# Layer 2 of a three-part fp32 kernel: loads of x2 in parts, another bend, longer transfers in the planner

## The chip, the cores and the metric

One NeuronCore of a Trainium2 chip runs the whole program. The metric is the device time of one execution in microseconds (us); before the change the median of 3 runs is 1015.37 us (1014.89 to 1016.47). Engines: PE (TensorE, matmuls), DVE (VectorE), ACT (ScalarE), POOL (GpSimd) and SP (SyncE, which issues DMAs).

## The reference

Attention over 4 batches, 8 heads, 576 positions, width 64, followed by two feed-forward layers on the 2304 tokens x 512 features that come out of it. All is float32.

```python
# attention: causal softmax, and a read of a memory, mixed by a gate
local = softmax(causal(q @ k.T / 8)) @ v
mem_out = (phi(q) @ M_prev) / (phi(q) @ z_prev + 1e-6)      # phi(x) = elu(x) + 1
x = g * mem_out + (1 - g) * local                           # 2304 x 512
# layer 1: w_in 512 x 2048, w_out 2048 x 512, scalars s and b
r = np.maximum(x @ w_in, 0.0)
x = (s * (r * r) + b) @ w_out
# layer 2: weights of the same shapes; the "bend"
h = x @ w_in
g = np.where(h >= 1, h, np.where(h <= -1, 0.0, (h + 1) ** 2 / 4))
out = g @ w_out
```

## The kernel before

Every fp32 operand of a matmul is kept as two halves, a rounded one (hi) and the rest (lo), and each product is three matmuls: hi·hi, hi·lo and lo·hi. Making the halves takes a rounding (`rnd`, ACT L536, DVE L537 or POOL L541) and a subtraction (`sub`, DVE L528 or POOL L532).

The order of all work comes from a planner in Python (`Plan`, L110 to 347). The kernel's code only records operations with their reads, writes, a priority (ATT before FFN before W2) and for each a list of "ways": the engines that could do it, with a cost in us. `Plan.order` simulates the engines with these costs, picks for each operation the engine, and gives one fixed order for each engine. An engine works strictly in that order: an instruction that waits holds up all behind it. The same holds for SP, whose queue issues nearly all DMAs (`dma`, L507; issued at L510): a DMA that must wait for a buffer or for data holds up the DMAs behind it. In the simulation, transfers follow one another at 335 GB/s, with 1.3 us ahead and 1.3 us behind each (DMA_START, DMA_END). Where the planner expects PE to stand idle it inserts small filler matmuls (L1298).

Layer 1 works on blocks of 256 tokens (the last, "wide", has 512) and leaves its result x2, scaled by s, in DRAM (x2d, one tensor for a block; L978). The term with b is the same for all tokens: b times the column sums of w_out. `column_sums` adds up the 32 halves of w_out in the tile mask (31 adds, L1032), sums over the partitions with four 128x1 matmuls (L1038) and keeps the result in cs (L1040).

Layer 2 works on 5 blocks of tokens (BLOCKS2: block 0 has 256 and is done plainly; blocks 1 to 4 have 512 and use Strassen's seven products), in two passes over the hidden units: FIRST, blocks 0, 1, 2, 3, 4 with half of the hidden units, then SECOND, blocks 4, 1, 2, 3, 0 with the other half. For each block `load_x2` (L1065) brings x2 from x2d to the tile xr, as one DMA for each block of layer 1 (two for a 512 token block); `x2_sums` (L1098) adds cs (ACT L1106 or POOL L1108), forms Strassen's sums (L1116, L1117) and makes their halves in xx (and gg). `products` (L1170 to 1172) multiplies with the weights in wi, `strassen` (L1181) combines the products in wif and wof, `bend` (L1142 to 1161) applies the bend and makes halves in wo and g, and `second` multiplies with w_out (L1202, L1203 with the rounded half, L1209 with the rest). The first pass stores its partial results (yd), the second loads them back (st<-yd), adds (DVE L1275) and stores out (out_dram<-st, L1278). During the first pass `prepare` (L664) converts the weights of the second: raw loads, roundings and subtractions (L594 to 605, L692, L714), stores to w2d; `bring` (L720) loads these later.

The bend before, for h in src: DVE clips h to -1..1 (L1152), ACT squares 0.5·clip + 0.5 (L521), DVE takes the larger of h (or clip) and the square (L1156, L1158).

Of the kernel before, what the change touches and what calls it, by code (L numbers as in the profile page):

```python
# [109 lines left out]
class Plan:  # L110
# [116 lines left out]
    def line(self, keys):  # L227
# [50 lines left out]
        while n_out < len(ops):  # L278
# [44 lines left out]
            if len(o.way) > 3:  # L323
                dma = max(dma, free[e] + self.DMA_START) + o.way[3]
                o.ends = ("SP", dma + self.DMA_END)
# [50 lines left out]
def tile_kernel(ctx: ExitStack, tc: tile.TileContext, qk_in, nv_in, z_prev, beta,  # L376
# [105 lines left out]
    R_RW = Pool([lambda i=i: made["xr"][:, i:i + 512] for i in (1024, 1536)] + [rr[:, 0:512]])  # L482
# [24 lines left out]
    def dma(dst, src, nbytes, r=(), w=(), pr=2, acq=(), late=False):  # L507
        small = pr in (ATT, LOAD)
        last = (nbytes / (240e3 if small else 335e3),)
# [154 lines left out]
    def prepare(p):  # L664
# [4 lines left out]
        def put(k, make):  # L669
# [7 lines left out]
            dma(lambda: w2d[p, k // 2][:, 512 * j:512 * j + 512], lambda: sg.t, P * 2048, [sg], [f"w2d{p}_{k // 2}"], W2)  # L677
# [23 lines left out]
        for i in range(2):  # L701
# [6 lines left out]
            for k in (8 + 2 * i, 9 + 2 * i):  # L708
# [272 lines left out]
    def layer1_step(bi, fi, ys):  # L981
# [6 lines left out]
        old = ["narrow"] * (wide and fi > 1)  # L988
        plan.phase = 1 if wide else None

        def rv(r=r):
# [4 lines left out]
            [hs] + old, [r], FFN, [r])  # L996
# [25 lines left out]
    def column_sums():  # L1022
# [16 lines left out]
        pe(1.0, go, ["mask", "sb"], [z], W2, [z])  # L1039
        dve(0.1, lambda: nc.vector.tensor_scalar(cs_t, z.t[:, 0:NK], con[:, 1:2], None, ALU.mult), [z, "sb"], ["cs"], W2)  # L1040
# [36 lines left out]

    def x2_plain():

        load_x2(0, lambda: made["xr"][:, 0:NK * T].rearrange("p (c n) -> p c n", c=NK))  # L1080
        for kt in range(NK):
# [6 lines left out]
            def lo(kt=kt):  # L1088
# [5 lines left out]
                ["xr", "cs"], [f"xp{kt}"], FFN)  # L1094
            dve(c_dve(T), lambda kt=kt, xv=xv, hi=hi, lo=lo: nc.vector.scalar_tensor_tensor(
                lo(), xv(), col(kt), f(hi()), ALU.add, ALU.subtract), ["xr", "cs"], [f"xp{kt}"], FFN)

    def x2_sums(bi):  # L1098
# [3 lines left out]
        load_x2(bi, xr)  # L1102
        for kt in range(NK):
            def xv(kt=kt):
# [4 lines left out]
                ["xr", "cs"], [f"xr{kt // 2}{j}" for j in range(2)], FFN)  # L1109
# [4 lines left out]
        def tt(i, j, a, c):  # L1114
# [251 lines left out]
```

## Time and profile before

| | |
|---|---|
| median of 3 runs | 1015.37 us (1014.89 to 1016.47) |
| the profiled execution | 1018.43 us, its span 1016.6 us |
| granted clock of PE, mean | 0.991 of full speed |
| busy: PE | 998.8 us, 98% of the span |
| DVE, ACT, POOL | 679.8, 571.0, 192.3 us |
| the chain that ended last | PE 86%, ACT 8%, DMA 3%, DVE 1% |

The profile is one execution, recorded by the hardware, and 3.06 us longer than the median of the timed runs. The span runs from the first to the last recorded instruction. "Busy" sums what an engine spent in instructions; PE's matmuls overlap, so a busy PE may still run at a low clock. The clock is given as a share of 2.4 GHz; its lower level is 1.2 GHz.

### The profile page before, as it was taken

What the parts mean: (1) busy time and instruction counts of PE and PEld (TensorE: products, weight loads), DVE (VectorE), ACT (ScalarE), POOL (GpSimd) and SP (SyncE); (2) the same over time, 40 slices, a digit from 0 to 9 for tenths busy, and PEclk for the clock granted to TensorE, in tenths of its full rate; (3) what the DMA queues carried; (4) which work ended last, traced back from release to release, by engine and by line L of the source; (5) the groups of instructions that cost most, each with busy time, mean ns of one, the idle gap of its engine ahead of it and who ended that gap; (6) DMA issues with size and microseconds to landing.
All of it is one profiled execution on the core that took longest, in us unless ns stands there. A gap on an engine that the chain in (4) does not pass through costs nothing.

```text
span 1016.6 us, 19496 instructions
## 1 busy us (share of the span) xinstructions
PE 998.8 (98%) x7484; PEld 882.8 (87%) x7484; DVE 679.8 (67%) x1597; ACT 571.0 (56%) x1301; POOL 192.3 (19%) x298
## 2 busy tenths in 40 slices
PE   8999999999999999999999999999999999989997
PEld 7799998898898898888998889989899899878886
DVE  5999855625744635644878967988797458666753
ACT  5999876746646655645565556555554233433322
POOL 5411133211110211101112213412321001211001
PEclk8999999999999999999999999999999999998999
DMA  9590034212122121220133347454426832130311
GB/s 324 195 410 21 22 95 139 73 35 81 46 74 62 61 66 50 84 66 21 71 118 105 125 151 241 145 161 154 154 94 243 314 127 86 40 125 1 104 31 32
DMA packets 50302, 115.57 MB, mean 114 GB/s; under 512 B 5024, under 2 KB 15776, under 8 KB 50208
## 3 DMA queue, kind: packets, MB, share of 16 engines
q1 hardware_dynamic: 49984, 113.72, 32.8%
q8 instruction: 59, 0.97, 0.4%
q0 software_dynamic: 224, 0.59, 0.3%
q14 instruction: 35, 0.29, 0.1%
HBM read 87.56 MB, written 26.74 MB: 112 GB/s over the span
## 4 chain that ended last, share of the span: by engine, by line
PE 86%; ACT 8%; DMA 3%; DVE 1%; issue 1%; SPq 0%; POOL 0%; DVEq 0%; ACTq 0%; POOLq 0%
PE hb L950 6%; PE hb L952 6%; PE hb L951 6%; PE ab L825 6%; PE yb L1013 5%; PE yb L1018 5%; PE yb L1014 5%; PE ab L904 4%; PE ab L880 4%; PE ab L1202 3%; PE yb L1202 3%; PE ab L1203 3%; PE yb L1203 3%; PE yb L1209 3%; PE ab L1209 3%; PE hb L1170 2%
## 5 line engine op out<-in xcount | busy, mean ns | idle before, releaser
L950 PE MATMUL hb<-xx,wi 128*128 128x256 f32 (+1 forms) x512 | 152.7, 298 | 0.1
L951 PE MATMUL hb<-xx,wi 128*128 128x256 f32 (+1 forms) x512 | 149.6, 292 | 0.0
L952 PE MATMUL hb<-xx,wi 128*128 128x256 f32 (+1 forms) x512 | 149.6, 292 | 0.0
L1013 PE MATMUL yb<-gg,wo 128*128 128x256 f32 (+1 forms) x394 | 102.4, 292 | 0.3 <-POOL gg L541 0.3
L950 PEld LDWEIGHTS hb<-xx,wi 128*128 128x128 f32 x512 | 96.3, 188 | 7.1 <-issue 3.5
L951 PEld LDWEIGHTS hb<-xx,wi 128*128 128x128 f32 x512 | 96.4, 188 | 2.8
L952 PEld LDWEIGHTS hb<-xx,wi 128*128 128x128 f32 x512 | 96.2, 188 | 2.9
L1014 PE MATMUL yb<-gg,wo 128*128 128x256 f32 (+1 forms) x394 | 98.0, 281 | 0.0
L528 DVE TENSOR_TENSOR gg<-rr,gg 128x256 fp32r<-128x256 f32 (+1 forms) x105 | 46.2, 442 | 76.0 <-ACT gg L536 56.4
L521 ACT ACTIVATE aa<-aa,sm 128x384 f32<-128x384 f32 (+4 forms) x112 | 69.4, 621 | 48.6 <-DVE sm L836 48.4
L521 ACT ACTIVATE wif<-wif,con 128x512 f32<-128x512 f32 x46 | 33.1, 721 | 87.4 <-DVE wif L1152 87.3
L836 DVE CUSTOM_DVE_ANT_0 aa<-ab,mask 128x512 f32<-128x512 f32 (+3 forms) x112 | 59.1, 553 | 32.9 <-PE ab L825 32.6
L1013 PEld LDWEIGHTS yb<-gg,wo 128*128 128x128 f32 x394 | 74.1, 188 | 7.4 <-issue 3.6
L1014 PEld LDWEIGHTS yb<-gg,wo 128*128 128x128 f32 x394 | 74.2, 188 | 0.4
L994 ACT ACTIVATE rr<-hb 128x256 f32<-128x256 f32 (+1 forms) x102 | 40.9, 401 | 56.7 <-PE hb L952 55.5
L1018 PE MATMUL yb<-gg,wo 128*128 128x256 f32 (+1 forms) x394 | 69.1, 288 | 0.0
L825 PE MATMUL ab<-qk 64*64 64x512 f32 (+5 forms) x320 | 58.3, 471 | 0.0
L1018 PEld LDWEIGHTS yb<-gg,wo 128*128 128x128 f32 x394 | 54.5, 188 | 2.2 <-issue 1.8
L1171 PE MATMUL ab<-xx,wi 128*128 128x256 f32 x192 | 54.1, 282 | 2.4 <-POOL xx L532 2.4
L1170 PE MATMUL ab<-xx,wi 128*128 128x256 f32 x192 | 54.0, 281 | 0.0
L1170 PE MATMUL hb<-xx,wi 128*128 128x256 f32 x192 | 54.0, 281 | 0.0
L1171 PE MATMUL hb<-xx,wi 128*128 128x256 f32 x192 | 54.0, 281 | 0.0
(337 smaller groups left out, 2838.4 us busy)
## 6 DMA issues: line engine op xcount, KB each, us to landing
w2d<-st SPq DMA_DIRECT2D x48, 256.0 KB, 3.4
nv<-in_nv_dram SPq DMA_DIRECT2D x16, 576.0 KB, 3.7
wir<-in_moe_w_in_dram SPq DMA_DIRECT2D x16, 512.0 KB, 10.2
wor<-in_moe_w_out_dram SPq DMA_DIRECT2D x16, 512.0 KB, 10.1
raw<-in_moe_w_in_dram SPq DMA_DIRECT2D x16, 512.0 KB, 3.6
raw<-in_moe_w_out_dram SPq DMA_DIRECT2D x16, 512.0 KB, 4.1
qk<-in_qk_dram SPq DMA_DIRECT2D x16, 448.0 KB, 3.3
xr<-x2d SPq DMA_DIRECT2D x14, 512.0 KB, 4.9
```

Of the source, the lines that this page charges most:

```text
L521: nc.scalar.activation(o(), i(), func, **{a: b() if callable(b) else b for a, b in kw.items()})
L825: nc.tensor.matmul(zs[x].t[own if t == 4 else slice(0, n), at:at + c1 - c0], qk.t[own, q0:q0 + n], qk.t[own, k0 + c0:k0 + c1], start=True, ...
L950: nc.tensor.matmul(o, w_in_part(fi, 0)[:, kt, :], x_h(kt), start=kt == 0, stop=False)
L951: nc.tensor.matmul(o, w_in_part(fi, 0)[:, kt, :], x_l(kt), start=False, stop=False)
L952: nc.tensor.matmul(o, w_in_part(fi, 1)[:, kt, :], x_h(kt), start=False, stop=kt == NK - 1)
L1013: nc.tensor.matmul(yv(c), w_out_part(fi, 0)[:, cs], gg.t[0], start=fi == 0 and c % k == 0, stop=False)
L1014: nc.tensor.matmul(yv(c), w_out_part(fi, 1)[:, cs], gg.t[0], start=False, stop=False)
L1018: pe(c_mm(n), lambda c=c, cs=cs, gg=gg, fi=fi: nc.tensor.matmul(yv(c), w_out_part(fi, 0)[:, cs], gg.t[1], start=False, stop=fi == NF - 1 a ...
L1170: nc.tensor.matmul(o, sw(q, k, 0, kt), xo(k, 0, kt), start=j == 0 and kt == 0, stop=False)
L1171: nc.tensor.matmul(o, sw(q, k, 0, kt), xo(k, 1, kt), start=False, stop=False)
L1202: nc.tensor.matmul(y.t, gh.t[:, cs], wo2(q, i, 0), start=first and jj == 0, stop=False)
L1203: nc.tensor.matmul(y.t, gh.t[:, cs], wo2(q, i, 1), start=False, stop=False)
```

## The change

Four edits, all in the source of one file; lines behind L1065 move down by 10.

1. The planner assumes longer transfers: 2.5 us more until the data of a w2d store or load, a yd store or load or a store of out count as landed, and 1.5 us more for a load of x2.
2. The load of a block of x2 into xr is split: for each of the two blocks of layer 1 one DMA for features 0 to 255 (256 KB) and two of 128 KB; and xr is tracked in 8 cells (feature chunk, token half) and no longer as one. Only the last chunk waits for the wide block of layer 1, whose spare buffers fall from three to two.
3. The bend: ACT makes relu(0.5·h + 0.5) and squares it, and DVE makes min(max(h, 1), square) in one operation.
4. The matmuls of the column sums get a higher priority, and one wait of the wide block's relu starts one step earlier.

```diff
@@ Plan.order
             if len(o.way) > 3:
                 dma = max(dma, free[e] + self.DMA_START) + o.way[3]
-                o.ends = ("SP", dma + self.DMA_END)
+                o.ends = ("SP", dma + self.DMA_END + o.way[4])
@@
-    R_RW = Pool([lambda i=i: made["xr"][:, i:i + 512] for i in (1024, 1536)] + [rr[:, 0:512]])
+    R_RW = Pool([lambda: made["xr"][:, 1536:2048], rr[:, 0:512]])
@@
-    def dma(dst, src, nbytes, r=(), w=(), pr=2, acq=(), late=False):
+    def dma(dst, src, nbytes, r=(), w=(), pr=2, acq=(), late=False, wait=0.0):
         small = pr in (ATT, LOAD)
-        last = (nbytes / (240e3 if small else 335e3),)
+        last = (nbytes / (240e3 if small else 335e3), wait)
@@ prepare: the store of w2d (one of two), and in the same way bring, the loads of yd, the stores of yd and out
-                dma(lambda k=k: w2d[p, k // 2][:, 512 * (k % 2):512 * (k % 2) + 512], lambda sg=sg: sg.t, P * 2048, [sg], [f"w2d{p}_{k // 2}"], W2)
+                dma(lambda k=k: w2d[p, k // 2][:, 512 * (k % 2):512 * (k % 2) + 512], lambda sg=sg: sg.t, P * 2048, [sg], [f"w2d{p}_{k // 2}"], W2, wait=2.5)
@@ layer1_step
-        old = ["narrow"] * (wide and fi > 1)
+        old, old_r = (["narrow"] * (wide and fi > x) for x in (1, 0))
...
-            [hs] + old, [r], FFN, [r])
+            [hs] + old_r, [r], FFN, [r])
@@ column_sums
-        pe(1.0, go, ["mask", "sb"], [z], W2, [z])
-        dve(0.1, lambda: nc.vector.tensor_scalar(cs_t, z.t[:, 0:NK], con[:, 1:2], None, ALU.mult), [z, "sb"], ["cs"], W2)
+        pe(1.0, go, ["mask", "sb"], [z], ATT, [z])
+        dve(0.1, lambda: nc.vector.tensor_scalar(cs_t, z.t[:, 0:NK], con[:, 1:2], None, ALU.mult), [z, "sb"], ["cs"], FFN)
@@
-    def load_x2(bi, view):
+    def cells(kts, js=(0, 1)):
+        return [f"xr{kt}_{j}" for kt in kts for j in js]
+
+    def load_x2(bi):
 
         p0, p1 = BLOCKS2[bi]
         for l1, (a, e) in enumerate(BLOCKS):
             s, t = max(a, p0), min(e, p1)
-            if s < t:
-                dma(lambda s=s, t=t: view()[:, :, s - p0:t - p0],
-                    lambda l1=l1, s=s, t=t, a=a: x2d[l1].rearrange("c p n -> p c n")[:, :, s - a:t - a],
-                    P * NK * (t - s) * 4, [f"x2d{l1}"] + ["wide"] * (bi > 0), ["xr"], W2)
+            if s >= t:
+                continue
+            if not bi:
+                dma(lambda: made["xr"][:, 0:NK * T].rearrange("p (c n) -> p c n", c=NK),
+                    lambda: x2d[0].rearrange("c p n -> p c n"), P * NK * T * 4, ["x2d0"], cells((0, 1)), W2, wait=1.5)
+                continue
+            for k0, k1 in ((0, 2), (2, 3), (3, 4)):
+                dma(lambda s=s, t=t, k0=k0, k1=k1: made["xr"].rearrange("p (c n) -> p c n", c=NK)[:, k0:k1, s - p0:t - p0],
+                    lambda l1=l1, s=s, t=t, a=a, k0=k0, k1=k1: x2d[l1].rearrange("c p n -> p c n")[:, k0:k1, s - a:t - a],
+                    P * (k1 - k0) * (t - s) * 4, [f"x2d{l1}"] + ["wide"] * (k0 == 3),
+                    cells(range(k0, k1), range((s - p0) // T, (t - p0) // T)), W2, wait=1.5)
@@ x2_sums: the bias add, and in the same way the other readers and writers of xr
-                ["xr", "cs"], [f"xr{kt // 2}{j}" for j in range(2)], FFN)
+                ["cs"], cells((kt,)), FFN)
@@ bend
-        clip = lambda: nc.vector.tensor_scalar(tmp(), src.t, -1.0, 1.0, ALU.max, ALU.min)
-        dve(c_dve(512, "cp" if h is None else "tt"), clip if h is None else alone(clip), [src, "wide"], [x], FFN, [x])
-        act(tmp, tmp, AF.Square, 512, ["sb"], [x], FFN, ap=1, scale=0.5, bias=con[:, 4:5])
+        act(tmp, lambda: src.t, AF.Relu, 512, [src, "sb", "wide"], [x], FFN, ap=1, acq=[x], psum=h is not None, scale=0.5, bias=con[:, 4:5])
+        act(tmp, tmp, AF.Square, 512, [], [x], FFN)
+        top = lambda: nc.vector.scalar_tensor_tensor(cv(), src.t, 1.0, tmp(), ALU.max, ALU.min)
         if h is None:
-            dve(c_dve(512), lambda: nc.vector.tensor_tensor(cv(), cv(), tmp(), ALU.max), [x], [c], FFN)
+            dve(c_dve(512), top, [x], [c], FFN)
         else:
-            dve(c_dve(512), alone(lambda: nc.vector.tensor_tensor(cv(), h.t, tmp(), ALU.max)), [h, x], [c], FFN, [c])
+            dve(c_dve(512), alone(top), [h, x], [c], FFN, [c])
```

The planner makes a new order from this. Up to PE's instruction 3862 of before, at 520.8 us in the trace, all engines' work is the same; behind it the order differs everywhere. Of operations there are 72 fewer on DVE in the bend and 72 more on ACT; POOL does 46 instead of 18 roundings of 512 columns and 11 instead of 21 subtractions of that size; ACT does 209 instead of 243 such roundings.

On SP, where the second pass loads x2 of block 2 (xr<-x2d), before:

```order
L510 DMA st_5815<-yd_126 128x512
L510 DMA xr<-x2d_120 128x4x256
L510 DMA out_dram<-st_5810 64x512 x2
L510 DMA out_dram<-st_5813 64x512 x2
L510 DMA st_5810<-yd_126 128x512
L510 DMA st_5813<-yd_126 128x512
L510 DMA out_dram<-st_5814 128x512
L510 DMA xr<-x2d_121 128x4x256
L510 DMA out_dram<-st_5812 128x512
```

and now:

```order
L510 DMA st_5812<-yd_126 128x512
L510 DMA xr<-x2d_121 128x2x256
L510 DMA xr<-x2d_120 128x2x256
L510 DMA xr<-x2d_121 128x256 x2
L510 DMA xr<-x2d_120 128x256 x2
L510 DMA out_dram<-st_5811 64x512 x2
L510 DMA out_dram<-st_5815 64x512 x2
L510 DMA st_5811<-yd_126 128x512
L510 DMA st_5815<-yd_126 128x512
```

The second of the two loads stood behind seven DMAs of out and yd; now all six parts of the block (two rows of 128x2x256, and two rows that stand for two parts each) are issued in a row, ahead of the stores of out. The same holds for block 3 of that pass.

On POOL, the operands xx of block 3 in the first pass, before (raw is the tile into which the raw weights are loaded):

```order
L541 TENSOR_SCALAR xx<-xr 128x512
L532 TENSOR_TENSOR xx<-xr,xx 128x512 x2
L541 TENSOR_SCALAR xx<-xr 128x512
L598 TENSOR_SCALAR raw_5809<-raw_5809 128x512
L532 TENSOR_TENSOR xx<-xr,xx 128x512 x2
```

and now (st holds weights that are being converted, gg the last of the operands):

```order
L541 TENSOR_SCALAR xx<-xr 128x512
L541 TENSOR_SCALAR st_5812<-st_5815 128x256
L532 TENSOR_TENSOR xx<-xr,xx 128x512
L715 TENSOR_TENSOR st_5810<-st_5811,st_5813 128x512
L541 TENSOR_SCALAR xx<-xr 128x512
L532 TENSOR_TENSOR gg<-xr,gg 128x512
L1127 TENSOR_TENSOR xr<-xr 128x2x256
L541 TENSOR_SCALAR xx<-xr 128x512 x2
```

The conversion of the raw tile no longer stands between the operands; steps of the conversion from st to st do.

On DVE, the last adds of the column sums (L1032), before:

```order
L605 SCALAR_TENSOR_TENSOR st_5814<-raw_5809,st_5814 128x512
L1032 TENSOR_TENSOR mask<-mask,wo_1588 128x512
L605 SCALAR_TENSOR_TENSOR st_5815<-raw_5807,st_5815 128x512
L528 TENSOR_TENSOR gg<-rr,gg 128x256
L692 TENSOR_TENSOR st_5813<-st_5810,st_5812 128x256
L1032 TENSOR_TENSOR mask<-mask,wo_1588 128x512
L528 TENSOR_TENSOR gg<-rr,gg 128x256
L1032 TENSOR_TENSOR mask<-mask,wo_1661 128x512 x2
L528 TENSOR_TENSOR gg<-rr,gg 128x256 x2
```

and now:

```order
L605 SCALAR_TENSOR_TENSOR st_5811<-raw_5808,st_5811 128x512
L1032 TENSOR_TENSOR mask<-mask,wo_1588 128x512
L528 TENSOR_TENSOR gg<-rr,gg 128x256
L1032 TENSOR_TENSOR mask<-mask,wo_1588 128x512
L692 TENSOR_TENSOR st_5812<-st_5811 128x256
L1032 TENSOR_TENSOR mask<-mask,wo_1661 128x512
L692 TENSOR_TENSOR st_5812<-st_5812,st_5810 128x256
L1032 TENSOR_TENSOR mask<-mask,wo_1661 128x512
```

The last add now stands ahead of the last conversions of raw weights (L603, L605). On PE the four matmuls L1038 moved with it, from the wide block's last groups to the place in front of the L1013 matmuls of an earlier group of layer 1.

## Rows read from the trace of the kernel before

**Rows 1.** what PE waited for, 500 us to the end: total us, times, longest

```profile
PE yb L1202 <- ACT wo L536: 5.2, 2, 3.6
PE ab L1171 <- POOL xx L532: 2.4, 1, 2.4
```

**Rows 2.** timeline of PE: start us, us, instruction [idle before <-releaser]

```profile
717.76 0.39 PE L1171 MATMUL ab<-xx,wi 128*128 128x256 f32 x1 [2.35 <-POOL xx L532]
...
719.14 0.60 PE L1202 MATMUL ab<-wo,wo 128*128 128x512 f32 x1
...
723.48 0.40 PE L1202 MATMUL yb<-wo,wo 128*128 128x512 f32 x1
...
868.63 0.50 PE L1202 MATMUL yb<-wo,wo 128*128 128x512 f32 x1 [1.59 <-ACT wo L536]
...
914.41 0.80 PE L1202 MATMUL yb<-wo,wo 128*128 128x512 f32 x1 [3.59 <-ACT wo L536]
...
921.01 0.39 PE L1202 MATMUL yb<-wo,wo 128*128 128x512 f32 x1
...
921.92 0.39 PE L1209 MATMUL yb<-wo,wo 128*128 128x512 f32 x1
```

**Rows 3.** stretches: us, busy us of each engine, granted clock, DMA share

```profile
718.00:723.00 5.00, 5.00 (x21) 4.15 (x21) 5.00 (x8) 1.97 (x3) 1.14 (x1) 0.66 0.00 0
914.40:921.20 6.80, 6.79 (x17) 5.37 (x18) 6.77 (x12) 3.08 (x5) 0.36 (x1) 0.55 0.00 0
```

**Rows 4.** timeline of POOL

```profile
715.20 0.85 POOL L598 TENSOR_SCALAR raw<-raw 128x512 int32<-128x512 uint32 x1 [2.00 <-DMA raw<-in_moe_w_out_dram]
```

**Rows 5.** chain of waits in 852 to 872 us: start us, us, what

```profile
860.41 5.09 DMA xr<-x2d
```

**Rows 6.** timeline of ACT

```profile
865.59 0.72 ACT L1106 ACTIVATE xr<-xr,cs 128x512 f32<-128x512 f32 x1 [3.19 <-DMA xr<-x2d]
...
910.96 1.33 ACT L1106 ACTIVATE xr<-xr,cs 128x512 f32<-128x512 f32 x2 [4.80 <-DMA st<-yd]
```

**Rows 7.** timeline of SP, loads of x2: start us, us in the queue

```profile
852.79 0.37 SPq L510 DMA_DIRECT2D xr<-x2d  x1
...
896.48 0.37 SPq L510 DMA_DIRECT2D xr<-x2d  x1
...
905.60 0.42 SPq L510 DMA_DIRECT2D xr<-x2d  x1
```

**Rows 8.** DMA, 500 us to the end: GB/s in 40 slices; issues, KB, us to landing

```profile
GB/s 169 160 81 88 116 163 123 85 197 321 90 281 86 135 274 28 177 158 128 123 11 354 286 366 297 31 0 130 115 1 62 182 3 0 97 108 0 61 21 42
...
out_dram<-st SPq DMA_DIRECT2D x12, 256.0 KB, 3.2
```

**Rows 9.** groups of DVE, 600 us to the end: busy us, mean ns

```profile
L1156 DVE TENSOR_TENSOR wif<-wif,wof 128x512 f32<-128x512 f32 x16 | 15.7, 979 | 2.9 <-ACT wof L521 2.8
L1152 DVE TENSOR_SCALAR wif<-wif 128x512 f32<-128x512 f32 x28 | 14.9, 531 | 0.1
L1156 DVE TENSOR_TENSOR wif<-wif,wif 128x512 f32<-128x512 f32 x21 | 14.3, 681 | 0.0
```

**Rows 10.** groups of ACT, same stretch

```profile
L521 ACT ACTIVATE wif<-wif,con 128x512 f32<-128x512 f32 x46 | 33.1, 721 | 87.4 <-DVE wif L1152 87.3
...
L536 ACT ACTIVATE wo<-wif 128x512 fp32r<-128x512 f32 x22 | 13.8, 628 | 7.2 <-DVE wif L1156 5.6 <-DVE wif L1158 1.6
```

**Rows 11.** groups of POOL, same stretch

```profile
L532 POOL TENSOR_TENSOR xx<-xr,xx 128x512 fp32r<-128x512 f32 x17 | 24.1, 1422 | 74.3 <-DVE wif L1181 41.0 <-DVE wof L1181 17.3 <-ACT xx L536 15.6
L541 POOL TENSOR_SCALAR xx<-xr 128x512 fp32r<-128x512 f32 x12 | 10.2, 848 | 50.9 <-PE ab L1172 46.9 <-PE hb L1172 3.5 <-POOL xr L1108 0.3
```

**Rows 12.** timeline of DVE

```profile
521.99 0.41 DVE L528 TENSOR_TENSOR gg<-rr,gg 128x256 fp32r<-128x256 f32 x1
522.33 1.40 DVE L1032 TENSOR_TENSOR mask<-mask,wo 128x512 f32<-128x512 f32 x2
```

**Rows 13.** timeline of PE

```profile
520.78 0.28 PE L1013 MATMUL yb<-gg,wo 128*128 128x256 f32 x1
```

More of the change, by code (lines that the diff above doesn't have):

```diff
@@ L676, in put @@
             make(lambda: sg.t.bitcast(F32R), sg, [sg])
-            dma(lambda: w2d[p, k // 2][:, 512 * j:512 * j + 512], lambda: sg.t, P * 2048, [sg], [f"w2d{p}_{k // 2}"], W2)
+            dma(lambda: w2d[p, k // 2][:, 512 * j:512 * j + 512], lambda: sg.t, P * 2048, [sg], [f"w2d{p}_{k // 2}"], W2, wait=2.5)
         def split(k, a, r):
@@ L724, in bring @@
             dma(lambda nm=nm, i=i: f(parts_t[nm, i]), lambda k=k: w2d[p, k // 2], P * 4096, [f"w2d{p}_{k // 2}"],
-                [f"{nm}h{i}", f"{nm}l{i}"], W2)
+                [f"{nm}h{i}", f"{nm}l{i}"], W2, wait=2.5)
     def x_keys(kt, c0, c1):
@@ L1078, in x2_plain @@
     def x2_plain():
-        load_x2(0, lambda: made["xr"][:, 0:NK * T].rearrange("p (c n) -> p c n", c=NK))
+        load_x2(0)
         for kt in range(NK):
@@ L1093, in x2_plain @@
                  ("POOL", c_pool(T), lambda kt=kt, xv=xv, hi=hi: nc.gpsimd.tensor_scalar(hi(), xv(), col(kt), 1.0, ALU.add, ALU.mult))],
-                ["xr", "cs"], [f"xp{kt}"], FFN)
+                cells((kt // 2,), (kt % 2,)) + ["cs"], [f"xp{kt}"], FFN)
             dve(c_dve(T), lambda kt=kt, xv=xv, hi=hi, lo=lo: nc.vector.scalar_tensor_tensor(
-                lo(), xv(), col(kt), f(hi()), ALU.add, ALU.subtract), ["xr", "cs"], [f"xp{kt}"], FFN)
+                lo(), xv(), col(kt), f(hi()), ALU.add, ALU.subtract), cells((kt // 2,), (kt % 2,)) + ["cs"], [f"xp{kt}"], FFN)
     def x2_sums(bi):
@@ L1101, in xr @@
             return made["xr"].rearrange("p (c n) -> p c n", c=NK)
-        load_x2(bi, xr)
+        load_x2(bi)
         for kt in range(NK):
@@ L1117, in tt @@
                  ("POOL", c_pool(512, "tt"), lambda: nc.gpsimd.tensor_tensor(o(), b(*a)(), b(*c)(), ALU.subtract))],
-                ["xr"] + [f"xr{i}{j}" for i, j in (a, c)], [f"xr{i}{j}"], FFN)
+                [x for h, g in (a, c) for x in cells((2 * h, 2 * h + 1), (g,))], cells((2 * i, 2 * i + 1), (j,)), FFN)
         def halves(k, i, j):
-            a, r = b(i, j), ["xr", f"xr{i}{j}"]
+            a, r = b(i, j), cells((2 * i, 2 * i + 1), (j,))
             def hi():
@@ L1252, in layer2 @@
             for c in range(ny):
-                dma(lambda c=c: parts[c].t, lambda c=c: yd[bi][c], P * DM * 4, [f"yd{bi}_{c}"], [parts[c]], W2, [parts[c]])
+                dma(lambda c=c: parts[c].t, lambda c=c: yd[bi][c], P * DM * 4, [f"yd{bi}_{c}"], [parts[c]], W2, [parts[c]], wait=2.5)
         if not same:
@@ L1271, in layer2 @@
                 rnd(lambda st=st: st.t, lambda c=c: ys[c].t, DM, [ys[c]], [st], FFN, True, [st])
-                dma(lambda c=c: yd[bi][c], lambda st=st: st.t, P * DM * 4, [st], [f"yd{bi}_{c}"], FFN)
+                dma(lambda c=c: yd[bi][c], lambda st=st: st.t, P * DM * 4, [st], [f"yd{bi}_{c}"], FFN, wait=2.5)
                 continue
@@ L1277, in layer2 @@
                 o = pos - p0 - c * P
-                dma(lambda tok=tok, m=m: out[tok:tok + m, :], lambda st=st, o=o, m=m: st.t[o:o + m, :], m * 2048, [st], [], FFN)
+                dma(lambda tok=tok, m=m: out[tok:tok + m, :], lambda st=st, o=o, m=m: st.t[o:o + m, :], m * 2048, [st], [], FFN, wait=2.5)
     for kind, *i in ORDER:
```

## The prediction

> **What bounds the kernel now.** I read the busy times first: the table of the profile gives PE 98% of the span, no other engine more than 67%. So time is saved only where PE waits or runs at a low clock, and the second view is the list of what PE waited for. From 500 us to the end it has two entries with three waits in all [rows 1]: two for a rounding on ScalarE, 5.2 us together, and one for a subtraction on GpSimd. The PE timeline has the places [rows 2]: 2.35 us idle before 717.76, 1.59 before 868.63, 3.59 before 914.41, that is 7.53 us. The third view is the clock behind them [rows 3]: granted 0.66 in 718 to 723 us and 0.55 in 914.4 to 921.2, so mostly the lower of its two levels (1.2 against 2.4 GHz), after PE had stood still. The full-clock pitch of a 512 column matmul is (921.92 - 921.01)/4 = 0.2275 us. Between 719.14 and 723.48 stand 12 of them: 4.34 - 2.73 = 1.61 lost. Between 914.41 and 921.01 stand 16: 6.60 - 3.64 = 2.96 lost. The pitch after 868.63 is the full one, nothing lost. The three places are worth 7.53 + 1.61 + 2.96 = 12.10 us.
>
> What each waits for: at 717.76 GpSimd had stood 2.00 us for a raw weight load, converted it, and only then took up the subtraction of an operand that PE wanted [rows 4]. At 868.63 ScalarE had stood 3.19 us, at the bias add of the second piece of x2 (L1106) [rows 6], in front of the bend's square and rounding; that piece was issued at 860.41 and took 5.09 us [rows 5], while the first had been issued at 852.79 [rows 7]. At 914.41 it is the same: ScalarE stands 4.80 us at L1106 [rows 6]. The releaser named there is a load of yd, but L1106 reads only x2; its second piece was issued on SP at 905.60, 9.12 us behind the first [rows 7], and 905.60 + 5.09 [rows 5] = 910.7.
>
> **The change part by part.** *x2 in parts (layer 2, second half).* Before, the second piece stands in SP's queue behind stores of out and loads of yd that wait for those stores. Now all pieces of a block stand together ahead of them. At 852.79 the whole of xr was free, since the first piece had to wait for all of it. Six issues at about 0.4 put the last at 855.0; with the 5.09 us of the 512 KB piece of rows 5 it lands at 860.1. PE was ready at 868.63 - 1.59 = 867.04 and its operand came 3.04 us behind ScalarE's start at 865.59, so landing by 863.9 is in time: 3.8 us to spare. At the other place: 896.48 + 2.2 + 5.1 = 903.8; PE was ready at 910.82, 3.45 us behind ScalarE's 910.96, so it needs 907.3: 3.5 us to spare. Both stalls go: 1.59 + 3.59 + 2.96 = 8.14 us. What is late next there is the bend itself, in front of which nothing of x2 stands any more. The stores that are passed come some 2 us later; their st buffers are wanted by the yd loads of a block later, with several us in hand as long as a block lasts 44 us (896.48 - 852.79). Bounds: 0 gained, if the landing is late all the same (a rival), to 8.14. I take 8.14, since both margins are larger than any piece's own 3.2 [rows 8].
>
> *The order around 717.* In the new order of that block no conversion of a fresh raw load stands ahead of GpSimd's subtraction, so 2.35 + 1.61 = 3.96 us go. But GpSimd now rounds more: 46 roundings of 512 columns where there were 18, mostly of xx, wo14 and wo15. In the block after it a copy of a raw load (L596) does stand between two operands; that load is issued long before, so I put 0.3 there, with bounds 0 and 2.35, the one wait of this kind.
>
> *The bend.* 72 bends. DVE loses a clip of 0.53 and turns its maximum of 0.68 into one operation of the same two tensors [rows 9]; 0.68 is the nearest row, 0.98 (same shape, other buffers) the upper end. ACT gains a second operation of 0.63 to 0.72 [rows 10]: 72 x 0.53 = 38 us less on DVE, 72 x 0.63 = 45 us more on ACT. DVE has 680 busy us and ACT 571 in 1017, and both lie beside PE, so the sums cost nothing; the latency does count where PE waits for a bend: before 0.53 + 0.72 + 0.68 = 1.93, now 0.72 + 0.63 + 0.68 = 2.03. A tenth of a microsecond, at the few places without slack: 0.3 in all. Bounds: -0.3 (DVE, freed in front of the roundings) and 72 x 0.1 = 7.2, if every bend were waited for; the three waits in rows 1 say that nearly none is.
>
> *Column sums.* Their four 128x1 matmuls move on PE from the end of layer 1 to the place in front of the group that starts at 520.78 [rows 13]. They need the last of the adds L1032, which ended at 522.33 + 1.40 = 523.73 [rows 12]. On DVE eight instructions now stand behind it that stood ahead, four of 256 columns at 0.34 from start to start (521.99 to 522.33) and four of 512 at 0.70: 4.2 us, so it ends at 519.6, 1.2 us before PE comes. Cost 0; at most 523.73 - 520.78 = 2.95 if the adds came as late as before. I add 0.2 for what shifts there on ACT. The longer transfers that the planner assumes issue nothing of their own; their effect is the order already counted.
>
> **Sum.** Profiled execution 1018.43 (its span 1016.6): -8.14 - 3.96 + 0.3 + 0.3 + 0.2 = -11.3, hence 1007.1. That execution was 3.06 us longer than the median of the runs shown. If the 3.06 have nothing to do with the stalls, the median falls by 11.3 to 1004.1; if they lie in the stalls, which are transfers and waits, it falls by 8.2 to 1007.2. I take 1005.5, a little nearer the first. A measurement here can tell 0.2%, 2.0 us, from no change.
>
> **Rivals.** *A, a stall comes back elsewhere.* For it: everything after 520.8 us is ordered anew, PE has no slack, and one of ACT's or GpSimd's in-order queues in front of a late transfer is all it takes. Against it: of 29 GpSimd roundings and subtractions of xx [rows 11] only one was waited for in rows 1. One such wait costs what the old ones cost with their clock: 3.96 (717) to 6.55 (914). From 1004.1 that is 1008 to 1010.7; two of them make 1012 to 1017, no change or nearly.
>
> *B, the parts land late: slower.* Place: SP's six issues at 852.79 and 896.48. If the pieces are served one after another at the 3.2 us of the 256 KB row [rows 8], the last lands at 852.79 + 19.2 = 872.0, where before it was 865.5, and at 915.7, where before it was 910.7: 6.5 + 5.0 us more idle, with 3.96 saved: 1015.4 + 11.5 - 4.0 = 1022.9. It decides when the last landing comes over 11 us after the first issue. Against it the throughput row [rows 8]: 512 KB in 5.09 us are 103 GB/s, slices reach 366 GB/s, so transfers of one queue overlap more than threefold. The Trainium skill, "DMA: Bandwidth & Descriptors" (Rules for kernel authors, and the anatomy of one DMA), speaks against the change as well: many small transfers are to be merged into one, each has a fixed part of about 2.0 us that is mostly waiting for completion. Its fit would make an estimate of 6 x 2.0 + 2.4 = 14.4 us if those fixed parts came in series, and a late landing; by the same page they are latency, which overlaps, and the trace's 366 GB/s agree with that.
>
> *C, GpSimd as the gate: slower.* Place: the 28 roundings that it takes over, where wo14, wo15 and xx go straight to PE. A rounding takes 0.848 there [rows 11] against 0.628 on ACT [rows 10], and a DVE operation of two tensors shows 0.98 beside 0.68 in a group of one shape [rows 9]. If both differences lay on PE's path every time, 28 x (0.22 + 0.30) = 14.6 us: 1004.1 + 14.6 = 1018.7. It decides at 11.3/28 = 0.40 us of lateness each; half of that still ends at 1010. Against it: PE waited for GpSimd once in this half of the program. The Trainium skill, "GPSIMD Engine Reference" (Specifications), states that GpSimd shares its SBUF interface with VectorE and contends with DVE instructions of two SBUF inputs; the 0.98 fits it, and no row before isolates it.
>
> **Chances.** The forecast 0.66, its own range 1003 to 1008 (1003.3 is all 12.1 gone at no cost). A with one stall 0.16, with two 0.04; B 0.06; C 0.08, of which half ends near 1010 and half slower. Range: from 1002.5 (the run-to-run half microsecond below 1003) to 1012, which takes in A with one stall and the mild C, and leaves out about 0.14 and the tails of the likeliest. Faster 0.66 + 0.16 + 0.04 = 0.86; same 0.05 (A with two stalls, part of C); slower 0.09.
>
> **What would show it.** Right: in the profile after, PE's list of waits past 500 us holds no entry for ACT wo or POOL xx above 0.5 us; the granted clock is 1.00 in every stretch of layer 2; L1106's line has no idle time before it on ACT that a transfer ended and PE then shares; the L1038 matmuls stand at 521 us with no wait. Wrong: an xr piece landing over 11 us after its block's first issue (B); PE waiting for POOL wo or xx in many small pieces (C); one long wait with a clock drop behind it at a new place (A); the last L1032 on DVE ending after 520.8.

## The result and the profile after

| | before | changed |
|---|---|---|
| median of 6 runs each | 1016.75 us (1014.89 to 1017.48) | 1005.59 us (1004.22 to 1006.76) |
| ratio, 95% interval | | 0.9891, 0.9878 to 0.9905 |
| profiled execution, its span | 1018.43, 1016.6 us | 1006.03, 1004.3 us |
| busy PE, DVE, ACT, POOL | 998.8, 679.8, 571.0, 192.3 us | 993.5, 659.4, 588.9, 204.6 us |

The change makes the kernel 1.1% faster, 11.2 us between the medians. What PE waited for from 500 us on (line, releaser, total us, times, longest), against [rows 1]:

```profile
PE yb L1013 <- ACT gg L536: 0.6, 1, 0.6
PE yb L1212 <- ACT wo L536: 0.4, 1, 0.4
```

The three waits are gone; 1.0 us in two small ones is left, 0.6 of it in layer 1 (at 511 us) and 0.4 at 719.94. The stretches of the changed kernel that answer to [rows 3], each about the place where PE had waited (us, busy us by engine, granted clock, DMA share, GB/s):

```profile
711.00:716.00 5.00, 5.00 (x45) 5.00 (x44) 4.88 (x7) 3.63 (x7) 4.15 (x4) 1.00 0.30 115
860.00:872.00 12.00, 12.00 (x73) 10.70 (x72) 9.02 (x15) 5.49 (x9) 2.27 (x3) 1.00 0.25 83
903.00:921.00 18.00, 18.00 (x110) 16.08 (x109) 10.15 (x17) 5.13 (x9) 2.07 (x3) 1.00 0.16 45
```

PE is busy for all of each, at a granted clock of 1.00, which is the upper level. SP's queue (start, time until the last of the group was issued), against [rows 7]:

```profile
847.36 2.55 SPq L510 DMA_DIRECT2D xr<-x2d  x5
851.66 3.55 SPq L510 DMA_DIRECT2D out_dram<-st  x4
...
879.00 12.56 SPq L510 DMA_DIRECT2D xr<-x2d  x6
```

For block 2 the last five of the six parts of x2 are issued from 847.36 on, all ahead of the four stores of out; for block 3 six from 879.00 to 891.56. In both blocks the first part goes out 10 us ahead of the other five (837.34 for block 2, 879.00 for block 3), which, with xr tracked in cells, waits only for its own. ScalarE, against [rows 6]:

```profile
852.40 0.72 ACT L1116 ACTIVATE xr<-xr,cs 128x512 f32<-128x512 f32 x1 [1.50 <-DMA xr<-x2d]
858.88 0.72 ACT L521 ACTIVATE wif<-wif,con 128x512 f32<-128x512 f32 x1 [5.75 <-DVE wif L1191]
...
891.84 0.72 ACT L1116 ACTIVATE xr<-xr,cs 128x512 f32<-128x512 f32 x1 [2.24 <-DMA xr<-x2d]
894.06 0.72 ACT L1116 ACTIVATE xr<-xr,cs 128x512 f32<-128x512 f32 x1 [1.49 <-DMA xr<-x2d]
900.53 0.72 ACT L521 ACTIVATE wif<-wof,con 128x512 f32<-128x512 f32 x1 [5.75 <-DVE wof L1191]
```

The bias add of x2 (now L1116) still waits for its transfer, 1.5 to 2.2 us, but 6 us before the bend's work of the same block comes (858.88, 900.53): between the two ACT has nothing to do (5.75 us idle each). The transfers themselves (issues, size, median us to landing; before, 14 of 512 KB took 4.9 us):

```profile
xr<-x2d SPq DMA_DIRECT2D x14, 256.0 KB, 3.1
xr<-x2d SPq DMA_DIRECT2D x24, 128.0 KB, 3.1
```

### The profile page after: what moved, and what is told of

The parts are those of the page before. It is cut to its first block, busy times and chain, and to the rows that moved or that the text cites. A ratio compares the mean times of both kernels' runs of the same rounds, so it can differ in the third digit from the quotient of the medians.

```text
span 1004.3 us, 19651 instructions
## 1 busy us (share of the span) xinstructions
PE 993.5 (99%) x7480; PEld 878.0 (87%) x7480; DVE 659.4 (66%) x1545; ACT 588.9 (59%) x1331; POOL 204.6 (20%) x320
## 4 chain that ended last, share of the span: by engine, by line
PE 91%; ACT 4%; DVE 2%; DMA 1%; issue 1%; POOL 0%; SPq 0%; DVEq 0%; POOLq 0%
PE hb L950 6%; PE hb L952 6%; PE hb L951 6%; PE ab L825 6%; PE yb L1013 5%; PE yb L1018 5%; PE yb L1014 5%; PE ab L904 4%; PE ab L880 4%; PE yb L1212 3%; PE yb L1213 3%; PE yb L1219 3%; PE ab L1219 3%; PE ab L1212 3%; PE ab L1213 3%; PE ab L1181 3%
## 5 line engine op out<-in xcount | busy, mean ns | idle before, releaser
L1013 PE MATMUL yb<-gg,wo 128*128 128x256 f32 (+1 forms) x394 | 102.7, 293 | 0.7 <-ACT gg L536 0.6
L1013 PEld LDWEIGHTS yb<-gg,wo 128*128 128x128 f32 x394 | 74.1, 188 | 8.1 <-issue 3.6
L994 ACT ACTIVATE rr<-hb 128x256 f32<-128x256 f32 (+1 forms) x105 | 43.8, 417 | 54.7 <-PE hb L952 52.1
L860 POOL TENSOR_SCALAR aa<-aa,sm 128x384 f32<-128x384 f32 (+4 forms) x41 | 25.3, 619 | 149.0 <-DVE sm L853 114.7
L1181 PE MATMUL ab<-xx,wi 128*128 128x256 f32 x196 | 55.2, 281 | 0.0
L1182 PE MATMUL ab<-xx,wi 128*128 128x256 f32 x196 | 55.1, 281 | 0.0
L1180 PE MATMUL ab<-xx,wi 128*128 128x256 f32 x196 | 55.1, 281 | 0.0
L1180 PE MATMUL hb<-xx,wi 128*128 128x256 f32 x188 | 52.8, 281 | 0.0
```

What stands on the lines that cost most here:

```text
L1013: nc.tensor.matmul(yv(c), w_out_part(fi, 0)[:, cs], gg.t[0], start=fi == 0 and c % k == 0, stop=False)
L1180: nc.tensor.matmul(o, sw(q, k, 0, kt), xo(k, 0, kt), start=j == 0 and kt == 0, stop=False)
L1181: nc.tensor.matmul(o, sw(q, k, 0, kt), xo(k, 1, kt), start=False, stop=False)
```

## Experiments on the order alone

Five kernels keep the planned order of one of the two kernels and move a few instructions in it. In all of them the helper code shifts line numbers by 11 to 15 (L1106 is L1119 there, L1202 is L1216 or L1217, and L1227 where the changed kernel is the base).

**The second load of x2 moved up.** `order` is the planner's list of all operations, `place` finds one of them; 10 and 12 are the first loads of blocks 2 and 3 in the second pass.

```diff
+    for n in (10, 12):
+        i, j = place("x2", n), place("x2", n + 1)
+        order.insert(i + 1, order.pop(j))
```

> The kernel before with its order kept, except that in the second pass the second load of x2 of blocks 2 and 3 is issued right behind the first one, ahead of the stores of out. No split, old bend, old column sums. Queue theory (the two stalls before 868.63 and 914.41 come from this load's place in SP's queue alone): both vanish, 1.59 + 3.59 us idle and 2.96 us of low clock, so about 8.1 us (0.80%) faster than before; PE's wait for POOL xx near 717 stays at 2.3. Bend theory (those stalls are the bend's long chain on ACT and DVE, which the new bend relieves): PE still waits for ACT wo at both places, less than 2 us gained.

Measured: 0.9919 (0.9898 to 0.9940) of before, 8.2 us. The waits:

```profile
PE ab L1185 <- POOL xx L543: 3.1, 1, 3.1
```

Both waits for ACT wo are gone, with two DMAs moved and the old bend. The wait near 717 stays (3.1 us in this execution). The bend theory fails here.

**One conversion on GpSimd moved behind an operand.** `low` 63 is the conversion (L598) of [rows 4], `xo5` the subtraction behind it.

```diff
+    j = place("low", 63)
+    go = order.pop(j)
+    order.insert(place("xo5", 2) + 1, go)
```

> The kernel before with its order kept, except that on GpSimd one conversion of raw weights stands behind the next subtraction of xx and no longer ahead of it (one instruction moved by one place). Queue theory: the wait of 2.35 us before 717.76 goes with its 1.61 us of low clock, about 4.0 us (0.39%) faster; the two waits for ACT wo stay at 1.6 and 3.6. Rival (the operand was late by itself, because its rounding on ACT came late): the wait stays above 1 us and less than 2 us are gained.

Measured: 0.9980 (0.9967 to 0.9994), 2.0 us (0.6 to 3.4): half of what was expected. The wait itself went as expected, from 2.35 to 0.5 us, but the two others grew, from 5.2 to 6.9 us, and a new one of 0.3 us stands at 719.59:

```profile
PE yb L1216 <- ACT wo L547: 6.9, 2, 4.8
PE ab L1185 <- POOL xx L543: 0.5, 1, 0.5
```

The loads of x2 in this kernel:

```profile
849.92 0.37 SPq L510 DMA_DIRECT2D xr<-x2d  x1
...
857.48 0.42 SPq L510 DMA_DIRECT2D xr<-x2d  x1
...
894.12 0.37 SPq L510 DMA_DIRECT2D xr<-x2d  x1
...
904.06 0.42 SPq L510 DMA_DIRECT2D xr<-x2d  x1
```

The first load is issued 2.9 us earlier than before [rows 7], as PE is ahead by that. The second follows 7.6 and 9.9 us behind the first of its block (7.6 and 9.1 before), since transfers stand between them (that PE's lead does not shorten these is my reading and was not tested), and its own transfer took 0.5 us longer at the first place. So 0.5 and 1.2 us come back at the next two places. In these two executions PE's waits from 500 us on add up to 7.7 us here and 7.6 before: none of the idle time was saved. What was kept is clock: behind the first place the granted clock is 1.00 (718 to 723 us), which spares the 1.61 us of low clock, and behind the third wait only seven matmuls run slowly (913.26 to 916.31) where sixteen did, 1.5 us less. Time saved ahead of a stall that waits for transfers can come back there.

**Both moves.**

```diff
+    order.insert(place("xo5", 2) + 1, go)
...
+        order.insert(i + 1, order.pop(j))
```

> The kernel before with both moves, three instructions in all, and nothing of the new planner, split, bend or column sums. Queue theory: 8.1 + 4.0 = 12.1 us (1.19%) faster, which equals the changed kernel within 0.2%. Rival (the changed kernel also gains from the freed VectorE and from the operations it does elsewhere): it stays at least 3 us slower than the changed kernel.

Measured: 1005.3 us, 0.9889 (0.9870 to 0.9909); the changed kernel has 0.9891. What PE waited for:

```profile
PE ab L1185 <- POOL xx L543: 0.3, 1, 0.3
PE ab L1223 <- DVE wo L539: 0.3, 1, 0.3
```

Three instructions at another place in the old order give as much as the whole change. What the split, the new bend and the column sums do beyond these stalls has no net effect that could be told here: the intervals reach 1.4 to 2.0 us to either side.

**The changed kernel with two of the six parts late.** They are the parts of the last feature chunk; `bias 3` is the bias add that reads them.

```diff
+    for n, ls in ((5, (3, 4)), (6, (5, 6))):
+        for l1 in ls:
+            go = order.pop(place(f"x2 {l1}", 5))
+            order.insert(place("bias 3", n), go)
```

> The changed kernel with its order kept, except that for blocks 2 and 3 of the second pass the two 128 KB pieces of the last feature chunk (two of the six parts) are issued behind stores of out and loads of yd again, where the second load stood before. Queue theory: ScalarE stands at the bias add of that chunk in front of the bend's work, PE waits again at both places; with one bias add behind the load instead of two, 5 to 8 us slower than the changed kernel (1010.5 to 1013.5). Bend theory: the new bend has room for this, less than 2 us slower.

Measured: 0.9975 (0.9960 to 0.9989) of before, so 8.5 us slower than the changed kernel (0.9975/0.9891 = 1.0085), a little more than the upper end. SP and ACT at the first place, and PE's waits:

```profile
857.50 0.91 SPq L510 DMA_DIRECT2D xr<-x2d  x2
```

```profile
861.63 0.72 ACT L1129 ACTIVATE xr<-xr,cs 128x512 f32<-128x512 f32 x1 [10.97 <-DMA xr<-x2d]
862.25 0.71 ACT L532 ACTIVATE wif<-wif,con 128x512 f32<-128x512 f32 x1
```

```profile
PE yb L1227 <- POOL wo L552: 5.0, 2, 2.5
```

ACT stands 10.97 us at the bias add (L1129 here) of a part issued at 857.50; the bend's first operation follows at 862.25, where the changed kernel has it at 858.88. GpSimd's rounding wo, which needs the bend's result, comes late by that, and PE waits for it. The new bend has no room for that.

**The old load, but its reader moved down on ACT.** This came last, after the planned kernels below had refuted a part of my theory.

```diff
+    acts = {id(o.way[2]) for o in plan.ops if o.way[0] == "ACT"}
+    for n, ks in ((5, (2, 3)), (6, (2, 1))):
+        late = [order.pop(place(f"bias {k}", n)) for k in ks]
+        j = place("bias 0", n)
+        left = 3
+        while left:
+            j += 1
+            left -= id(order[j][0]) in acts
+        order[j + 1:j + 1] = late
```

> The kernel before with its order kept on every engine but ACT: for blocks 2 and 3 of the second pass the two bias adds of x2 (L1106) stand behind the bend's square and the two roundings wo that follow them, and no longer ahead. The second load of x2 is as late as before. Two-queue theory (a late load costs only what stands behind its reader on ACT): both waits go, 8 us (0.8%) faster than before, as with the load moved up; GpSimd's wait near 717 stays. Load theory (the landing itself holds PE): the waits stay at 1.6 and 3.6.

Measured: 0.9925 (0.9901 to 0.9948), 7.6 us, the same as with the load moved up. SP and ACT at the second place:

```profile
904.26 0.42 SPq L510 DMA_DIRECT2D xr<-x2d  x1
```

```profile
906.75 0.63 ACT L547 ACTIVATE wo<-wif 128x512 fp32r<-128x512 f32 x1 [0.77 <-PE hb L1187]
907.35 0.63 ACT L547 ACTIVATE wo<-wof 128x512 fp32r<-128x512 f32 x1
909.40 1.34 ACT L1119 ACTIVATE xr<-xr,cs 128x512 f32<-128x512 f32 x2 [1.41 <-DMA xr<-x2d]
```

The load is issued as late as ever (904.26), ACT waits 1.41 us for it at 909.40, and PE does not notice, since both roundings wo are done by then. Only GpSimd's wait near 717 is left, 2.4 us.

## Experiments on the parts of the change, planned anew

Medians are from several sets of runs; the ratios to the kernel before in the same set are what compares. For the split alone, of which I expected at least 8.1 us, there is no time: what it does without the other edits is not shown.

| edits that are in | median, us | ratio to before, interval |
|---|---|---|
| all (the changed kernel) | 1005.59 | 0.9891 (0.9878 to 0.9905) |
| bend alone | 1010.74 | 0.9935 (0.9915 to 0.9956) |
| longer transfers alone, not for x2 | 1013.86 | 0.9966 (0.9953 to 0.9979) |
| all but the bend | 1013.20 | 0.9958 (0.9946 to 0.9971) |
| all but the split | 1004.81 | 0.9878 (0.9861 to 0.9895) |
| all but the column sums | 1006.73 | 0.9898 (0.9881 to 0.9916) |
| all but the longer transfers | 1006.17 | 0.9892 (0.9877 to 0.9907) |
| longer transfers and column sums | 1008.58 | 0.9917 (0.9897 to 0.9937) |

**The bend alone** (the hunk of `bend`).

```diff
+        act(tmp, lambda: src.t, AF.Relu, 512, [src, "sb", "wide"], [x], FFN, ap=1, acq=[x], psum=h is not None, scale=0.5, bias=con[:, 4:5])
+        act(tmp, tmp, AF.Square, 512, [], [x], FFN)
...
```

> The kernel before with the new bend alone (edit 3), planned anew. The second load of x2 of blocks 2 and 3 still stands behind five and four DMAs of out and yd. Queue theory: PE still waits at both places, the gain is below 4 us (what GpSimd's place near 717 gives, 0 to 4). Bend theory: with VectorE freed by 38 us the three waits go, 8 us faster or more.

Measured: 6.6 us faster, between the two theories. One wait is left, 3.4 us:

```profile
854.44 0.39 SPq L510 DMA_DIRECT2D xr<-x2d  x1
...
899.64 0.43 SPq L510 DMA_DIRECT2D xr<-x2d  x1
```

```profile
858.75 2.03 POOL L1108 TENSOR_SCALAR xr<-xr,cs 128x512 f32<-128x512 f32 x3 [17.63 <-DMA xr<-x2d]
862.08 0.62 POOL L541 TENSOR_SCALAR wo<-wif 128x512 fp32r<-128x512 f32 x1 [1.30 <-DVE wif L1154]
...
904.36 2.46 POOL L1108 TENSOR_SCALAR xr<-xr,cs 128x512 f32<-128x512 f32 x3 [21.59 <-DMA xr<-x2d]
907.67 0.62 POOL L541 TENSOR_SCALAR wo<-wif 128x512 fp32r<-128x512 f32 x1 [0.85 <-DVE wif L1154]
```

```profile
908.34 0.62 PE L1202 MATMUL yb<-wo,wo 128*128 128x512 f32 x1 [3.44 <-POOL wo L541]
```

The late load now holds up POOL, which has the bias adds (L1108) and behind them the rounding wo. For block 2 the load went out at 854.44 and the rounding was done at 862.7, in time. For block 3 it went out at 899.64, L1108 began at 904.36, the rounding at 907.67, and PE stood until 908.34. So the expectation, a wait at both places, was wrong; the new plan put one load far enough up, and the raw conversion before an operand at 711.04, where PE did not wait.

**The longer transfers alone** (all `wait=2.5`, and `o.way[4]`).

```diff
+                o.ends = ("SP", dma + self.DMA_END + o.way[4])
...
```

> The kernel before with the planner's longer transfers alone (edit 1; for x2's loads nothing, since they come with the split), planned anew. The second load of x2 stands behind seven and five DMAs of out and yd, as before. Queue theory: both waits for ACT wo stay, less than 4 us faster. Rival (the planner, told of the real length of transfers, plans around them): 8 us faster or more.

Measured: 3.5 us faster, within the queue theory; PE waits 2.4 and 3.4 us for ACT wo at the two places, and not for GpSimd.

**All but the bend.**

```diff
-        act(tmp, tmp, AF.Square, 512, [], [x], FFN)
+        clip = lambda: nc.vector.tensor_scalar(tmp(), src.t, -1.0, 1.0, ALU.max, ALU.min)
...
```

> The changed kernel with the old bend (all but edit 3), planned anew; its six parts of x2 stand ahead of the stores. Queue theory: within 3 us of the changed kernel (1004 to 1009), since 38 us of VectorE off PE's path buy nothing. Bend theory: 5 us slower than the changed kernel or more.

Measured: 6.8 us slower than the changed kernel (0.9958/0.9891), as the bend theory had it. But the time is not lost where a bend is. The first matmul of Strassen's products and the last matmuls of the program, here and in the changed kernel:

```profile
643.96 0.28 PE L1180 MATMUL ab<-xx,wi 128*128 128x256 f32 x1
...
1006.26 1.08 PE L1251 MATMUL yb<-wo,g 128*128 128x512 f32 x4
```

```profile
636.75 0.28 PE L1180 MATMUL ab<-xx,wi 128*128 128x256 f32 x1
...
998.95 1.08 PE L1251 MATMUL yb<-wo,g 128*128 128x512 f32 x4
```

From the one to the other, with the same matmuls between them, it is 362.3 us with the old bend and 362.2 with the new one. The loss of 7.2 us lies ahead of that. This plan differs from the first instructions on: counted by the columns of its matmuls, without the fillers, PE comes to 20,000 columns at 54.2 us where the changed kernel does at 47.7, and stays 5.7 to 6.0 us behind from 50,000 to 500,000; one wait of 1.7 us follows in layer 1 (0.6 in the changed kernel). The clock does not account for it: up to 50 us PE is busy 42.4 instead of 45.0 us, at a mean granted clock of 0.96 against 0.93. What does is not shown. So in Strassen's blocks the bend costs and gives nothing, and the median of a kernel that is planned anew does not tell that by itself.

**All but the split.**

```diff
-            for k0, k1 in ((0, 2), (2, 3), (3, 4)):
+                dma(lambda s=s, t=t: view()[:, :, s - p0:t - p0],
...
```

> The changed kernel without the split (all but edit 2; x2's loads keep the 1.5 us), planned anew. The second load of x2 of blocks 2 and 3 stands behind eight and six DMAs of out and yd. Queue theory: PE waits again for ACT or GpSimd wo at both places, 6 to 11 us slower than the changed kernel (1011.5 to 1016.5), and what is lost lies in layer 2. Rival (any new plan with the new bend does as well): within 3 us of the changed kernel.

Measured: 1004.8 us, as fast as the changed kernel (the intervals overlap). My expectation was wrong. The second load is late all the same:

```profile
858.58 0.50 SPq L510 DMA_DIRECT2D xr<-x2d  x1
```

It is issued 8.8 us behind the first (849.74). But on ACT:

```profile
859.45 0.72 ACT L521 ACTIVATE wif<-wif,con 128x512 f32<-128x512 f32 x1 [10.93 <-DVE wif L1181]
...
863.04 0.64 ACT L521 ACTIVATE wof<-wof 128x512 f32<-128x512 f32 x1
863.58 0.71 ACT L1106 ACTIVATE xr<-xr,cs 128x512 f32<-128x512 f32 x1
```

The bias add stands behind the bend's operations, and finds its data there. For block 3 it still waits for its transfer, 2.9 us (908.23), but behind the bend's operations, and PE does not wait there. This led to the theory that two queues are needed for the stall: a late load on SP, and its reader ahead of PE's operands on ACT or POOL; the kernel above with only the reader moved tests it.

**Longer transfers and column sums, without split and new bend.**

```diff
+                    P * NK * (t - s) * 4, [f"x2d{l1}"] + ["wide"] * (bi > 0), ["xr"], W2, wait=1.5)
```

> Edits 1 and 4 with 1.5 us for x2's loads, without the split and with the old bend, planned anew. The second load of x2 stands behind ten and seven DMAs of out and yd, later than before, but on ACT the bias adds no longer stand ahead of the bend's roundings. Two-queue theory (what the planner knows of the load is enough): no wait for wo, within 3 us of the changed kernel (1003 to 1009) apart from the first 50 us. Load theory: 6 to 11 us slower than the changed kernel. Bend theory: 5 us slower or more, with waits spread over the bends.

Measured: 0.26% above the changed kernel by the ratios, 3.0 us by the medians, the upper part of what the two-queue theory gave. There is no wait for wo, but one of 2.4 us for the rounding g: a bias add (L1106, at 910.45, its load issued at 906.58) stands ahead of that on ACT. The kernel with the longer transfers alone, which lacks the 1.5 us for x2 and the column sums, stays at 0.9966.

**All but the column sums; all but the longer transfers.**

```diff
-        pe(1.0, go, ["mask", "sb"], [z], ATT, [z])
+        pe(1.0, go, ["mask", "sb"], [z], W2, [z])
...
```

> The changed kernel with the old priorities of the column sums (all but edit 4), planned anew; the parts of x2 stand ahead of the stores. If the move of the four matmuls costs what layer 1 lost in the trace (0.9 us from the first matmul of layer 1 to the first of Strassen's products), this is 0 to 2 us faster than the changed kernel (1003.5 to 1005.5) and would be the fastest version; if the matmuls had hindered something at the end of layer 1, it is 1 us slower or more.

```diff
-                o.ends = ("SP", dma + self.DMA_END + o.way[4])
+                o.ends = ("SP", dma + self.DMA_END)
```

> The changed kernel with the planner's old lengths of transfers (all but edit 1), planned anew; the parts of x2 still stand ahead of the stores. Queue theory: both places stay without a wait, so it is within 3 us of the changed kernel unless a conversion of raw weights stands ahead of an operand again (then up to 4 more). Rival (the longer transfers are what makes the order right): 6 us slower or more, with waits at DMAs of out, yd or w2d.

Measured: 1006.7 and 1006.2 us, both the same as the changed kernel within the intervals; neither waits at the two places. What the column sums' move costs or gives cannot be told: the 0.9 us that I took for its cost lies inside the intervals. The wait for gg in layer 1 is there without the move too (1.1 us); its cause is shown in the next section. No version was shown to beat the changed kernel: the fastest median, without the split, is 0.8 us lower, inside the noise.

## Why the prediction was right

*Where the time was.* Three waits with their clock, 12.1 us: confirmed by moving three instructions, which gave 0.9889, or 11.3 us of 1016.75 (9.2 to 13.2).

*x2 in parts, 8.14 us.* Right in size: 8.2 us with the load moved up, 8.5 lost with two parts late. The margin was there: the bias adds end 5.75 us before the bend needs ACT, where I had worked out 3.8 and 3.5 us to spare. The parts do not go out six in a row, as I had it: the first is 10 us ahead of the others. The step was incomplete in its cause. I took the load's place on SP for the reason; it is one of two, and moving its reader on ACT does as well (7.6 us). Which of the two the planner changes is open to it: with the split it moved the load, without the split the reader.

*The order around 717, 3.96 us.* The wait went, but by itself it was worth 2.0 us (0.6 to 3.4), since its idle time came back, 1.7 us of it at the two places behind. In the sum it counts in full, because those were gone too. GpSimd's order there now:

```profile
711.42 1.29 POOL L532 TENSOR_TENSOR gg<-xr,gg 128x512 fp32r<-128x512 f32 x1
...
715.21 1.64 POOL L541 TENSOR_SCALAR xx<-xr 128x512 fp32r<-128x512 f32 x2
716.82 0.66 POOL L596 TENSOR_SCALAR st<-raw 128x512 f32<-128x512 f32 x1
```

No raw conversion stands between the operands, and its copy (716.82) comes behind them. The 0.3 us that I put for a wait of that kind did not occur.

*The bend, 0.3 us.* About right: 362.3 against 362.2 us from Strassen's first product on. The group of DVE's new operation (busy us, mean ns):

```profile
L1164 DVE SCALAR_TENSOR_TENSOR wif<-wif,wif 128x512 f32<-128x512 f32 x22 | 16.9, 770 | 0.5 <-ACT wif L521 0.2
```

The mean is 0.77 us where I took 0.68, but it mixes two cases. The 41 of these operations beside which GpSimd had nothing to do took 0.68 to 0.69 us each; two in this group took 1.79 and 1.32 us, beside a GpSimd operation on two tensors. The 0.98 us that I took for other buffers [rows 9] is a mean of the same kind (see the last section).

*Column sums, 0.2 us.* The four matmuls L1038, which the trace counts as eight, wait for nothing. The adds end at 520.45 + 0.68 = 521.13 and PE comes at 522.00: 0.9 us in hand, 1.2 predicted.

```profile
520.45 0.68 DVE L1032 TENSOR_TENSOR mask<-mask,wo 128x512 f32<-128x512 f32 x1
```

```profile
522.00 0.95 PE L1038 MATMUL ab<-con,mask 128*128 128x1 f32 x8
```

Up to the first product the changed kernel takes 0.9 us more from its first matmul of layer 1 on than before, 0.6 of it the wait for gg in the list above. That wait comes from the split. SP and ACT of the changed kernel:

```profile
502.36 1.39 SPq L510 DMA_DIRECT2D xr<-x2d  x3
```

```profile
509.70 0.66 ACT L594 ACTIVATE st<-raw 128x512 f32<-128x512 f32 x1 [1.05 <-DMA raw<-in_moe_w_in_dram]
```

Three loads of x2 stand here ahead of the loads of raw weights, where it was one; ACT stands 1.05 us at the conversion (L594) of these weights, and the rounding gg stands behind that. The five kernels with the split all show such a wait at this conversion, 0.46 to 4.80 us, and PE waits in four of them; none of the nine without the split shows one. So the orders differ earlier than at 520.8 us, as the section on the change has it: on SP from 502.8 us on, on DVE from 511.

*The sum.* Predicted for the profiled execution 1007.1, measured 1006.03; for the median 1005.5, measured 1005.59. That the median was hit to 0.1 us is luck. The gain that I forecast from 1015.37 is 9.9 us, the measured one is 11.2; the kernel before had 1016.75 over six runs, 1.4 more than over the three that I started from. Of my two cases the first was right: the 11.3 us that I had for the profiled execution came in the medians (11.2; the profiled executions differ by 12.4). Strassen's first product and the last matmuls of the kernel before, against 636.75 and 998.95 in the changed kernel:

```profile
635.61 0.28 PE L1170 MATMUL ab<-xx,wi 128*128 128x256 f32 x1
...
1010.08 1.07 PE L1241 MATMUL yb<-wo,g 128*128 128x512 f32 x4
```

That is 374.5 us before and 362.2 now: 12.3 us gone where the three waits with their clock make 12.1. Ahead of it the changed kernel is 1.1 us later, and behind it 1.2 us shorter; my sum had neither, and they cancel. Of the 0.8 us of small costs that I added none showed where I had put it.

*The rivals.* A occurred only in small: the wait for gg is of this kind, 0.6 us with no drop of the clock (1.00 from 500 to 520 us). B did not: the parts took 3.1 us each, and the last of the five that go out from 847.36 to 849.91 was read at 852.40. The sign that I had named for B did occur, a landing over 11 us after its block's first issue: 15 us in both blocks. It was a bad sign, because the first part now goes out 10 us ahead of the others; counted from the last issue it is 2.5 us. The Trainium skill, "DMA: Bandwidth & Descriptors" (anatomy of one DMA), gives a fixed part of about 2.0 us for each DMA, for those that GpSimd issues; my estimate for B took it over for loads that SP issues. The same 3.1 us for 128 and 256 KB agree with a fixed part, and five issued within 2.55 us overlapped. C did not cost PE: roundings on GpSimd took 0.73 to 0.80 us in the mean of each group (0.85 for xx in [rows 11]), yet PE waited for none of them.

## What to carry to other kernels

Before a late transfer is moved up or split, look at the instruction that waits for it: what stands behind that one on its engine is what is late, and moving either of the two is enough. Time saved ahead of a stall that waits for transfers can come back there, so take the last stall first, or all of them. Where a planner orders the whole program, a part undone and planned anew also changes what has nothing to do with it; keep the order and move single instructions, or compare one stage between two of its own instructions.

## What the runs showed of the hardware

A DVE operation on two tensors in SBUF took 1.78 us, where it takes 0.68 alone, when a GpSimd subtraction had begun just before it. In the kernel before, the 47 of the 64 such operations of the bend (L1156) that ran beside no GpSimd instruction took 0.67 to 0.69 us each; the four of 1.78 us each began 0.08 us after a GpSimd subtraction of two tensors and ended 0.55 us behind its end. One of them, DVE and POOL:

```profile
760.05 1.78 DVE L1156 TENSOR_TENSOR wif<-wif,wof 128x512 f32<-128x512 f32 x1
```

```profile
759.97 1.31 POOL L532 TENSOR_TENSOR xx<-xr,xx 128x512 fp32r<-128x512 f32 x1 [0.56 <-ACT xx L536]
```

The length of a wait alone did not tell whether PE's clock fell behind it. After the waits of 2.35 us (before, 717.76) and 2.53 us (two parts late, 866.80) stretches show 0.66 and 0.72; after 2.07 us (conversion moved, 866.22) and 2.40 us (longer transfers alone, 864.77) they show 1.00.

The first 35 us vary between kernels that begin with the same instructions: PE waited 1.6 to 4.6 us for the first loads of q and k, and the first matmul of layer 1 came between 31.6 and 34.1 us. Two single executions can differ by that much, 2.5 us, before layer 1 begins.
